# Attention and soft MoE on one core: the x transposes behind the routing, two masks in one matmul, and GpSimd's subtractions ahead of both spreads

## Chip, cores, metric

The kernel runs on one core of a Trainium2 chip. The metric is the device time of one execution in microseconds; lower is better. The core has the engines PE (matmul, with its weight loads PEld), VectorE (DVE), ScalarE (ACT), GpSimd (POOL) and SyncE (SP), which here issues transfers. Each engine runs its instructions in the order in which they are written; semaphores hold an instruction until what it needs is there.

## What is computed

Eight batches of causal attention with 12 heads of 448 positions and 64 dimensions; its output x (3584 x 768) goes through a soft mixture of 8 experts with 4 slots each. All is fp32.

```python
scores = scale * np.matmul(q, k.transpose(0, 1, 3, 2))
scores = np.where(mask, -1000000000.0, scores)
attn = np.exp(scores - np.max(scores, axis=-1, keepdims=True))
attn = attn / (np.sum(attn, axis=-1, keepdims=True) + 1e-09)
x = np.matmul(attn, v)               # heads side by side: (3584, 768)
logits = x @ phi                     # (3584, 32)
d = np.exp(logits - logits.max(0))   # over all positions
slot_input = (d / (d.sum(0) + 1e-09)).T @ x
h = np.maximum(slot_input[e] @ w1[e], 0.0); slot_out[e] = h @ w2[e]
c = np.exp(logits - logits.max(1, keepdims=True))
out = (c / (c.sum(1, keepdims=True) + 1e-09)) @ slot_out
```

## The kernel before

The attention part is a loop over 48 blocks, `block(p)` (lines 505 to 590); a block finishes one pair of heads, a = 2p and a + 1, and prepares the next pair. Six blocks are one batch; `m6 = p % 6`. Every instruction is kept in program order, so the order of the code is the order of each engine's queue.

Scores are kept transposed (keys in the partitions) in one of three PSUM buffers `s_[0..2]` of two banks each, head i in `s_[i % 3]`. They are made in two passes, since q and k are split into a rounded part and a rest. `scores1_all(i)` writes the causal masks with matmuls of the bf16 tile `tri` against an identity, and adds the products of the rounded parts for the four key chunks k3 (64 columns), k2 (192), k1 (320) and k0 (448). `max_keys(i, 0..2)` reduces the finished first pass on VectorE to a maximum per query (tile `r`: one large reduction with a transpose, two small ones). `max_row` transposes that on PE into `rt` and takes the last maximum on VectorE (`mr`). `max_spread` spreads it on GpSimd into the first 14 rows of `r2`. `scores2(i)` then adds with four matmuls the rests of q and the subtracted maximum. `exps` makes the exponential on ScalarE (`pt`). `attv` and `attv3` multiply by v: 64 matmuls for a pair, into `po`. `norm` divides on VectorE: steps 0 and 1 make the reciprocal `sm` of the row sums, step 2, in the next block, writes x.

For the routing, `xtrans(p)` transposes x of a pair by four PE transposes into the bank of `po`, and ScalarE copies it to `xts`. `next_logits` multiplies two pairs' `xts` by phi, and VectorE adds that to `lt`; `logits_b`, `logits_d` and `logits_e` keep the running maximum and exponentials, `dispatch_a/b` sum x into the slots' inputs `si`. These use the score buffer `m = s_[(a + 1) % 3]`, which is free at the end of a block and becomes the buffer of the head after next.

The casts are ScalarE's: `cast_q` and `cast_k` round q and k into `qd` and `ks`, two buffers each, and `copy_k2` copies rounded k to `k2`. The rests are GpSimd's: `sub_k(p + 2)` and `sub_q(p + 2)`, into `ks` and `r2`. Raw q and k come by `load_qk` on SP's queue into four rotating buffers; a load waits there for the subtraction that read the buffer last, and v and a weight tile are loaded by the same queue ahead of them. `misc()` hands out one PSUM bank, used for `rt`.

In block p, PE's order is: `scores2(a)`, `scores1_all(a + 2)`, `xtrans(p - 1)`, `scores2(a + 1)`, `scores1_all(a + 3)`, `rt` of a + 2, the 64 products, `rt` of a + 3, then logits, dispatch or neither by `m6`. Behind the last block come the experts, which read weights as they are loaded, and the combination and output.

Of the kernel before, what the change touches and what calls it, by code (L numbers as in the profile page):

```python
# [17 lines left out]
P = 128  # L18
# [62 lines left out]
def attention_soft_moe(ctx: ExitStack, tc: tile.TileContext, qk, va, phi, w1, w2, out):  # L81
# [91 lines left out]
    for hs in (slice(0, 1), slice(1, 2)):  # L173
# [11 lines left out]
    nc.gpsimd.memset(ident, 0.0)  # L185
    nc.gpsimd.affine_select(out=ident, in_=ident, compare_op=ALU.not_equal, fill=1.0,
                            base=0, pattern=[[-1, P]], channel_multiplier=1)
    tri = const.tile([P, P], BF16, name="tri")
    nc.gpsimd.memset(tri, 0.0)
    nc.gpsimd.affine_select(out=tri, in_=tri, compare_op=ALU.is_ge, fill=NEG,  # L190
                            base=0, pattern=[[1, P]], channel_multiplier=-1)

    pob = ps_1.tile([P, 512], F32, name="po")
    po2 = pob[:, 0:NQ * VC].rearrange("p (a b)->p a b", b=VC)
# [14 lines left out]
    def misc(name):  # L209
        return ps_1.tile([P, 512], F32, tag="m", name=name)  # L210
# [37 lines left out]
    def scores1(i, part):  # L248
        if i >= NHD:
            return  # L250
        p, h = divmod(i, 2)
        ks, qd = ks_[p % NR], qd_[p % NR]
        if ("s", i) not in st:
            st["s", i] = s_[i % 3]
            st["open"] = set()
        s = st["s", i]

        bank = part in ("c12", "k1", "k2")
        start = bank not in st["open"]
        st["open"].add(bank)  # L260
        if part[0] == "k":
            c = int(part[1])
            o, w, m = S * h + P * c, S - CQ0[c], min(P, S - P * c + (KP if i else 0))
            nc.tensor.matmul(s[0:m, SCOL[c]:SCOL[c] + w], ks[:, o:o + m],
                             qd[:, h, CQ0[c]:S], start=start, stop=False, skip_group_check=True)
            return
        if part == "c12":
            o = s[:, SC1:SC1 + 2 * SC2].rearrange("p (a n) -> p a n", n=SC2)[:, :, 0:P]
            mask = tri.unsqueeze(1).to_broadcast([P, 2, P])
        else:  # L270
            w = P if part == "c0" else S - 3 * P
            o, mask = s[:, SCOL[int(part[1])]:SCOL[int(part[1])] + w], tri[:, 0:w]
        nc.tensor.matmul(o, identb, mask, start=start, stop=False, skip_group_check=True)

    def scores1_all(i):
        for part in ("c0", "c3", "k3", "c12", "k2", "k1", "k0"):
            scores1(i, part)

    def max_keys(i, k):
# [20 lines left out]
    def max_row(i, k, w=RW - RF):  # L300
        if i >= NHD:
            return
        if k == 0:
            st["rt", i] = misc(f"rt{i}")
            nc.tensor.transpose(out=st["rt", i][0:w, 0:P], in_=r_[i % 2][:, RF:RF + w], identity=ident)
        else:
            mr = st["mr", i] = wk.tile([NQB, 32], F32, tag="mr", name=f"mr{i}", bufs=2)
            nc.vector.tensor_reduce(out=mr, in_=st.pop(("rt", i))[0:NQB, 0:P].rearrange("p (g t)->p t g", g=4),
                                    axis=AX.X, op=ALU.max, negate=True)

    def max_spread(i):
        if i >= NHD:
            return
        p, h = divmod(i, 2)
        mr = st.pop(("mr", i))

        nc.gpsimd.affine_select(out=r2_[p % NR][0:NQB, h].rearrange("p (b t)->p b t", t=32),
                                in_=mr.unsqueeze(1).to_broadcast([NQB, NQB, 32]),
                                compare_op=ALU.is_equal, fill=0.0, base=0,
                                pattern=[[-1, NQB], [0, 32]], channel_multiplier=1)  # L320
# [144 lines left out]
    later = [lambda: nc.gpsimd.memset(mk, 0.0), lambda: nc.gpsimd.memset(mk[96:P, 64:P], -1.0e30),  # L465
             lambda: nc.gpsimd.memset(run_m[1], 3.0e38), lambda: nc.gpsimd.memset(run_z, 0.0),
             lambda: nc.gpsimd.memset(si, 0.0), lambda: nc.gpsimd.memset(sid, 0.0)]
    later += [lambda g=g: sid_part(g) for g in range(4)]
    later += [lambda: nc.gpsimd.memset(nm[:, 0:NSLOT], 0.0)]

    later += [lambda: nc.gpsimd.tensor_copy(out=srep, in_=sid.unsqueeze(1).to_broadcast([P, 4, NSLOT]))]

    warm(START[0], a=x_[1][:, NCH - 1, 0:AW].bitcast(BF16))
    h0, h1 = slice(0, 1), slice(1, 2)
# [9 lines left out]
        max_keys(0, k)  # L484
    cast_k(0, h1)
    cast_q(0, h1)
    sub_k(0, h1, nc.vector)
    max_row(0, 0)
    max_row(0, 1)
    max_spread(0)  # L490
    warm(START[2])
    scores1_all(1)
# [1 line left out]
    copy_k2(0, h0)  # L494
    cast_k(1, h0)
    cast_k(1, h1)
    cast_q(1, h0)
    sub_k(1, h0)
    sub_k(1, h1)
    for k in range(3):  # L500
# [4 lines left out]
    def block(p):  # L505
        a, b = 2 * p, p // 6 - 1
        last, m6 = p == NPAIR - 1, p % 6
        if p + 1 < NPAIR:
            loads_v(p + 1, nc.sync if p + 1 < NPAIR - 1 else nc.scalar)
        if p % 2 and p // 2 < RES - 1 or p == 2 * RES - 2:  # L510
            load_w(p // 2)
        load_qk(p + 3, 0)

        if p:
            norm(p - 1, 2)
        scores2(a, range(NCH))
        exps(a)
        if p == 0:
            max_row(1, 0)
            max_row(1, 1)  # L520
            max_spread(1)
            copy_k2(0, h1)
            cast_q(1, h1)
            sub_q(1)
        scores1_all(a + 2)
        for k in range(3):
            max_keys(a + 2, k)
        if p:
            cast_q(p + 2)
            xtrans(p - 1)  # L530
        scores2(a + 1, range(NCH))
        exps(a + 1)
        if p == 0:
            cast_k(2)
            cast_q(2)
# [12 lines left out]
        max_spread(a + 2)  # L548
        if p == 0:
            sub_q(2)  # L550
# [23 lines left out]
        m = s_[(a + 1) % 3]  # L574
        if m6 in (3, 5) and p > 6:
            dispatch_a(b, m6 // 5, m)
            dispatch_b(b, m6 // 5, m)
        elif m6 == 1 and p > 6:
            logits_e(b, m)
        elif m6 in (2, 4):  # L580
            next_logits(p // 6, m6 - 2, m)
            if p == NPAIR - 2:
                dispatch_a(b, 1, m[:, 512:1024])
                dispatch_b(b, 1, m[:, 512:1024])
        elif m6 == 0 and p:
            next_logits(b, 4, m)
            logits_b(b, lt)

    for p in range(NPAIR):
        block(p)  # L590
# [316 lines left out]
```

## Time and profile before

| | |
|---|---|
| median of 3 runs (lowest to highest) | 426.62 us (426.61 to 427.95) |
| the profiled execution: time, span | 427.31 us, 425.4 us |
| attention blocks | from 10.2 us to about 329 us of the span |
| share of the span, DVE, ACT, POOL | 70%, 67%, 62% |
| DMA, mean | 280 GB/s |
| ScalarE: exponential of one head, copy of `xts` | 1.03 us, 0.59 us |
| GpSimd: subtraction for a pair, spread of one head | 2.08 us, 0.64 us |

A row of the timeline has the start in microseconds from the span's start, the duration, the engine, line and operation, the tiles (out<-in), sizes and a count of instructions merged; in brackets stands how long the engine was idle before and what released it. All operations go through one helper, so all have line 65, and are told apart by their tiles. `s<-r,k` is `scores2`, `s<-tri,identb` are the masks, `s<-qd,ks` is `scores1`, `po<-ident,x` are the x transposes, `s<-xts,phi` the logits and `s<-x,gs` the dispatch. A matmul's duration includes its way through the array: starts of successive rows tell its pace.

### The profile page before, as it was taken

To read this page: it belongs to the slowest core of one execution; us is meant where nothing else is said; L and a number is where in the kernel's file an instruction comes from. 1 tells how busy PE (TensorE), PEld (TensorE's weight loads), DVE (VectorE), ACT (ScalarE), POOL (GpSimd) and SP (SyncE) were. 2 spreads that over 40 slices of the span, in tenths; PEclk is the share of its full clock that TensorE was granted. 3 is DMA by queue.
4 is the path that set the end of the run, shared out by engine and by line. 5 is a ranking of instruction groups with operands and counts; after the bars stand their busy time and mean duration, and the time that the engine had idled before them with its cause. 6 is when DMAs were issued, how large, how long until landed. Compare 5 with 4: busy or idle time off the path is not lost.

```text
span 425.4 us, 14150 instructions
## 1 busy us (share of the span) xinstructions
PE 382.2 (90%) x5752; PEld 288.2 (68%) x5752; DVE 296.9 (70%) x817; ACT 283.6 (67%) x400; POOL 265.8 (62%) x215
## 2 busy tenths in 40 slices
PE   6689999999999999999999999999997998998840
PEld 3577878777877778787787777787876654543430
DVE  7667787787787877878778788787785477423440
ACT  5778888788877978788788788787953111333330
POOL 7998888787887887888879787887851000000000
PEclk9999999999999999999999999999999999999995
DMA  7777786787767777668767777776769999999997
GB/s 274 244 226 250 251 280 182 243 267 249 241 204 242 256 266 251 222 219 273 257 232 210 237 264 230 260 254 197 285 230 331 378 422 422 425 418 414 394 384 319
DMA packets 34480, 119.17 MB, mean 280 GB/s; under 512 B 3824, under 2 KB 8944, under 8 KB 32880
## 3 DMA queue, kind: packets, MB, share of 16 engines
q1 hardware_dynamic: 34272, 118.01, 78.4%
q8 instruction: 45, 0.74, 0.7%
q10 hardware_dynamic: 144, 0.27, 0.2%
q14 instruction: 19, 0.16, 0.1%
HBM read 107.25 MB, written 11.01 MB: 278 GB/s over the span
## 4 chain that ended last, share of the span: by engine, by line
PE 66%; DVE 18%; DMA 4%; issue 2%; ACT 1%; POOL 0%; DVEq 0%
PE po L65 29%; PE s L65 23%; DVE x L65 7%; PE rt L65 5%; DMA w<-in_w_dram 4%; PE so L65 2%; DVE si L65 2%; PE pp L65 2%; PE hp L65 2%; DVE lm L65 2%; DVE sm L65 1%; DVE mr L65 1%; DVE lg L65 1%; PE cp L65 1%; PE e L65 1%
## 5 line engine op out<-in xcount | busy, mean ns | idle before, releaser
L65 ACT ACTIVATE pt<-s 128x1024 f32<-128x1024 f32 x96 | 98.5, 1026 | 57.1 <-PE s L65 50.9
L65 DVE TRANSPOSE_TENSOR_REDUCE r<-s 128x32 f32<-128x1024 f32 x96 | 120.0, 1250 | 22.1 <-PE s L65 18.1
L65 POOL TENSOR_TENSOR r<-qk,qd 64x896 fp32r<-64x896 f32 (+1 forms) x48 | 100.0, 2083 | 11.8 <-ACT qd L65 6.5
L65 POOL TENSOR_TENSOR ks<-qk,ks 64x896 fp32r<-64x896 f32 (+1 forms) x48 | 98.9, 2060 | 4.2 <-ACT ks L65 0.5
L65 PE MATMUL po<-va,pt 128*64 128x65 f32 x3040 | 99.4, 223 | 0.2 <-ACT xts L65 0.2
L65 PEld LDWEIGHTS po<-va,pt 128*64 128x64 f32 x3040 | 92.8, 138 | 6.2 <-ACT xts L65 0.4
L65 POOL TENSOR_SCALAR_AFFINE_SELECT r<-mr 14x448 fp32r<-14x448 f32 x96 | 61.4, 640 | 39.9 <-DVE sm L65 30.2
L65 PE MATMUL s<-qd,ks 128*128 128x448 f32 (+4 forms) x384 | 78.2, 315 | 0.7 <-POOL ks L65 0.4
L65 PE MATMUL s<-r,k 128*128 128x448 f32 (+3 forms) x384 | 69.7, 303 | 3.5 <-POOL r L65 3.5
L65 PEld LDWEIGHTS s<-r,k 128*128 128x128 f32 (+1 forms) x384 | 55.9, 176 | 19.3 <-issue 12.5
L65 PEld LDWEIGHTS s<-qd,ks 128*128 128x128 f32 (+2 forms) x384 | 49.7, 181 | 1.0 <-POOL ks L65 0.6
L65 ACT ACTIVATE ks<-qk 128x896 fp32r<-128x896 f32 (+1 forms) x50 | 46.0, 922 | 6.3 <-DMA qk<-in_qk_dram 2.6
L65 DVE TENSOR_REDUCE mr<-rt 14x32 f32<-14x128 f32 x96 | 24.8, 258 | 36.4 <-PE rt L65 36.3
L65 ACT ACTIVATE qd<-qk 128x896 fp32r<-128x896 f32 (+1 forms) x50 | 45.9, 918 | 1.0 <-DMA qk<-in_qk_dram 1.0
L65 ACT ACTIVATE k<-ks 64x896 fp32r<-64x896 f32 (+1 forms) x49 | 45.8, 935 | 1.1
L65 PE MATMUL s<-tri,identb 128*128 128x128 bf16 (+2 forms) x288 | 42.7, 235 | 2.7
L65 PE MATMUL po<-ident,x 128*128 128x128 f32 x188 | 30.7, 286 | 8.1 <-DVE x L65 6.2
L65 DVE TENSOR_REDUCE r<-r 128x16 f32<-128x32 f32 x192 | 33.7, 176 | 5.0
L65 PEld LDWEIGHTS po<-ident,x 128*128 128x128 f32 x188 | 19.8, 140 | 22.5 <-DVE x L65 22.4
L65 PE MATMUL rt<-ident,r 128*76 128x128 f32 x96 | 27.5, 287 | 2.6 <-DVE r L65 2.5
L65 ACT ACTIVATE xts<-po 128x512 f32<-128x512 f32 x47 | 27.9, 594 | 2.4 <-PE po L65 1.3
L65 PEld LDWEIGHTS <-identb 128*128 128x128 bf16 x309 | 24.1, 99 | 6.8 <-issue 5.8
(138 smaller groups left out, 364.1 us busy)
## 6 DMA issues: line engine op xcount, KB each, us to landing
qk<-in_qk_dram SPq DMA_DIRECT2D x94, 448.0 KB, 5.0
w<-in_w_dram SPq DMA_DIRECT2D x43, 768.0 KB, 6.1
w<-in_w_dram SPq DMA_DIRECT2D x10, 1536.0 KB, 20.4
va<-in_va_dram SPq DMA_DIRECT2D x47, 260.0 KB, 2.9
out_dram<-ot SPq DMA_DIRECT2D x16, 384.0 KB, 6.7
out_dram<-ot SPq DMA_DIRECT2D x2, 1536.0 KB, 9.3
qk<-in_qk_dram SPq DMA_DIRECT2D x4, 224.0 KB, 3.4
hw<-in_w_dram SPq DMA_DIRECT2D x1, 768.0 KB, 6.3
```

Of the source, the lines that this page charges most:

```text
L65: return self._tc.keep_in_program_order(op(*args, **kwargs))
```

## The change

It has five parts.

- `xtrans(p - 1)` moves to the end of the block, behind logits and dispatch, and writes the bank of `misc()`; its copy is a function of its own, `xcopy`, called a block later behind `exps(a)`. The logits of a pair follow a block later, so `m6` shifts by one for all routing steps; the last block gets one set of logits and two copies more.
- `max_row(a + 3, 0)` goes ahead of `attv3`, the last 16 of the 64 products, and writes columns 512 to 639 of `m` instead of the bank of `misc()`.
- The masks of chunks 0 and 3 are one matmul of 192 columns, with a tile `tri2` that holds both; k3 comes behind both mask matmuls.
- GpSimd subtracts q of pair p + 1 and then k of pair p + 2, both ahead of the block's two spreads; the cast of q moves behind the second exponential and the copy of k2, and q's load behind its subtraction.
- At the start, GpSimd's work on `sid` and `srep` moves to the last block, two halves of casts are put together or moved, and k of pair 2 is subtracted on VectorE.

```diff
-    tri = const.tile([P, P], BF16, name="tri")
+    tri2 = const.tile([P, AW + P], BF16, name="tri2")
+    tri = tri2[:, AW:AW + P]
...
-            w = P if part == "c0" else S - 3 * P
-            o, mask = s[:, SCOL[int(part[1])]:SCOL[int(part[1])] + w], tri[:, 0:w]
+            o, mask = s[:, SC3:SC3 + AW + P], tri2
...
-        for part in ("c0", "c3", "k3", "c12", "k2", "k1", "k0"):
+        for part in ("c03", "c12", "k3", "k2", "k1", "k0"):
...
     def xtrans(p):
-        x = st.pop(("x", p))
+        x, xm = st.pop(("x", p)), misc(f"xm{p}")
+        st["xm", p] = xm
         for c in range(NCH):
-            nc.tensor.transpose(out=pob[:, P * c:P * c + P], in_=x[:, c], identity=ident)
+            nc.tensor.transpose(out=xm[:, P * c:P * c + P], in_=x[:, c], identity=ident)
+
+    def xcopy(p):
         xt = st["xt", p] = xtp.tile([P, 512], F32, tag="xt", name=f"xts{p}", bufs=XT)
-        nc.scalar.activation(out=xt, in_=pob, func=AF.Copy)
+        nc.scalar.activation(out=xt, in_=st.pop(("xm", p)), func=AF.Copy)
...
-        load_qk(p + 3, 0)
-
+
+        if last:
+            for f in last_of:
+                f()
...
+        elif p > 1:
+            xcopy(p - 2)
         scores1_all(a + 2)
...
-        if p:
-            cast_q(p + 2)
-            xtrans(p - 1)
+        if p == 0:
+            cast_k(2, h0)
         scores2(a + 1, range(NCH))
...
-        sub_k(p + 2)
-        load_qk(p + 4, 1)
+        sub_q(p + 1)
+        load_qk(p + 3, 0)
         if p:
-            sub_q(p + 2)
-        max_row(a + 2, 0)
-        if m6 == 1 and p > 6:
+            sub_k(p + 2)
+            load_qk(p + 4, 1)
+        if m6 == 2 and p > 6:
             logits_d(b, lt)
         copy_k2(p + 1)
+        cast_q(p + 2)
         cast_k(p + 3)
+        max_row(a + 2, 0)
...
+        if p == 0:
+            sub_k(2, eng=nc.vector)
+            load_qk(4, 1)
         begun = set()
         if last:
+            next_logits(p // 6, 2, s_[(a + 2) % 3])
+            xtrans(p - 1)
+            xcopy(p - 1)
...
+        m = s_[(a + 1) % 3]
+        max_row(a + 3, 0, AW, m[:, 512:512 + P])
         attv3(p)
-        max_row(a + 3, 0, AW)
...
+        if m6 == 1 and p > 1:
             next_logits(b, 4, m)
             logits_b(b, lt)
+        elif m6 == 2 and p > 6:
+            logits_e(b, m)
+        elif m6 in (3, 5):
+            next_logits(p // 6, m6 - 3, m)
+        if m6 in (3, 4) and p > 6:
+            mm = m[:, 640:1024] if m6 == 3 else m[:, 0:384]
+            dispatch_a(b, m6 - 3, mm)
+            dispatch_b(b, m6 - 3, mm)
+        if p:
+            xtrans(p - 1)
```

In PE's queue, at the middle of block 4 before the change (`s_86` takes the first pass of head 10, `s_85` the second pass of head 9), the x transposes stand between the two heads:

```order
L65 MATMUL s_86<-qd_91,ks_92 128x192
L65 MATMUL s_86<-qd_91,ks_92 128x320
L65 MATMUL s_86<-qd_91,ks_92 128x448
L65 MATMUL po<-ident,x_94 128x128 x4
L65 MATMUL s_85<-r_90,k_97 128x448
L65 MATMUL s_85<-r_90,k_97 128x320
L65 MATMUL s_85<-r_90,k_97 128x192
L65 MATMUL s_85<-r_90,k_97 66x64
```

At the same place of the changed kernel, the second head's `scores2` follows directly:

```order
L65 MATMUL s_86<-tri_129,identb 128x2x128
L65 MATMUL s_86<-qd_91,ks_92 66x64
L65 MATMUL s_86<-qd_91,ks_92 128x192
L65 MATMUL s_86<-qd_91,ks_92 128x320
L65 MATMUL s_86<-qd_91,ks_92 128x448
L65 MATMUL s_85<-r_90,k_97 128x448
L65 MATMUL s_85<-r_90,k_97 128x320
L65 MATMUL s_85<-r_90,k_97 128x192
```

Nothing of the routing is left between the two heads, and k3 (66x64) now precedes k2.

PE's queue at the end of block 4, which has logits, before (the last of the 64 products, `rt` of the second head, logits of two pairs, next block):

```order
L65 MATMUL po<-va_93,pt_99 64x65
L65 MATMUL po<-va_93,pt_101 64x65
L65 MATMUL rt_710<-ident,r_96 64x128
L65 MATMUL s_85<-xts_556,phi_151 32x128 x4
L65 MATMUL s_85<-xts_650,phi_152 32x128 x4
L65 MATMUL s_86<-r_98,k_97 128x448
```

In the changed kernel, in block 5, which has logits now, `rt` of the second head stands between two runs of products:

```order
L65 MATMUL po<-va_100,pt_99 64x65 x12
L65 MATMUL po<-va_100,pt_101 64x65 x12
L65 MATMUL s_87<-ident,r_96 64x128
L65 MATMUL po<-va_100,pt_99 64x65
L65 MATMUL po<-va_100,pt_101 64x65
```

and at that block's end, from the last product on, stand:

```order
L65 MATMUL po<-va_100,pt_101 64x65
L65 MATMUL s_87<-xts_607,phi_154 32x128 x4
L65 MATMUL s_87<-xts_701,phi_155 32x128 x4
L65 MATMUL xm_788<-ident,x_94 128x128 x4
L65 MATMUL s_85<-r_90,k_97 128x448
```

The second head's `rt` stands 16 products earlier, in the score buffer, and the x transposes are the block's last work.

GpSimd's queue over one block and a half, before (`ks` and `r` with `qk` are the subtractions of k and q, `r<-mr` the spreads):

```order
L65 TENSOR_TENSOR ks_92<-qk_5_374,ks_92 64x896
L65 TENSOR_TENSOR r_98<-qk_5_427,qd_91 64x896
L65 AFFINE_SELECT r_90<-mr_579 14x448
L65 AFFINE_SELECT r_90<-mr_618 14x448
L65 TENSOR_TENSOR ks_89<-qk_6_468,ks_89 64x896
L65 TENSOR_TENSOR r_90<-qk_6_531,qd_88 64x896
```

And of the changed kernel:

```order
L65 TENSOR_TENSOR r_90<-qk_4_345,qd_88 64x896
L65 TENSOR_TENSOR ks_92<-qk_5_348,ks_92 64x896
L65 AFFINE_SELECT r_90<-mr_540 14x448
L65 AFFINE_SELECT r_90<-mr_578 14x448
L65 TENSOR_TENSOR r_98<-qk_5_437,qd_91 64x896
L65 TENSOR_TENSOR ks_89<-qk_6_440,ks_89 64x896
```

The subtraction of q is now that of pair 4 beside k of pair 5, and stands first; it writes the `r2` buffer that the block's spreads write too.

More of the change, by code (lines that the diff above doesn't have):

```diff
@@ L187, in attention_soft_moe @@
                             base=0, pattern=[[-1, P]], channel_multiplier=1)
-    tri = const.tile([P, P], BF16, name="tri")
-    nc.gpsimd.memset(tri, 0.0)
-    nc.gpsimd.affine_select(out=tri, in_=tri, compare_op=ALU.is_ge, fill=NEG,
-                            base=0, pattern=[[1, P]], channel_multiplier=-1)
+    tri2 = const.tile([P, AW + P], BF16, name="tri2")
+    tri = tri2[:, AW:AW + P]
+    nc.gpsimd.memset(tri2, 0.0)
+    for t in (tri2[:, 0:AW], tri):
+        nc.gpsimd.affine_select(out=t, in_=t, compare_op=ALU.is_ge, fill=NEG,
+                                base=0, pattern=[[1, t.shape[1]]], channel_multiplier=-1)
     pob = ps_1.tile([P, 512], F32, name="po")
@@ L298, in max_keys, with max_row @@
                                     axis=AX.X, op=ALU.max)
-    def max_row(i, k, w=RW - RF):
+    def max_row(i, k, w=RW - RF, to=None):
         if i >= NHD:
@@ L303, in max_row @@
         if k == 0:
-            st["rt", i] = misc(f"rt{i}")
+            st["rt", i] = misc(f"rt{i}") if to is None else to
             nc.tensor.transpose(out=st["rt", i][0:w, 0:P], in_=r_[i % 2][:, RF:RF + w], identity=ident)
@@ L466, in attention_soft_moe @@
              lambda: nc.gpsimd.memset(run_m[1], 3.0e38), lambda: nc.gpsimd.memset(run_z, 0.0),
[L467 to L471, printed above, removed]
+             lambda: nc.gpsimd.memset(si, 0.0)]
+    last_of = [lambda: nc.gpsimd.memset(sid, 0.0)]
+    last_of += [lambda g=g: sid_part(g) for g in range(4)]
+    last_of += [lambda: nc.gpsimd.memset(nm[:, 0:NSLOT], 0.0)]
+    last_of += [lambda: nc.gpsimd.tensor_copy(out=srep, in_=sid.unsqueeze(1).to_broadcast([P, 4, NSLOT]))]
     warm(START[0], a=x_[1][:, NCH - 1, 0:AW].bitcast(BF16))
@@ L486, in attention_soft_moe @@
     cast_q(0, h1)
-    sub_k(0, h1, nc.vector)
     max_row(0, 0)
     max_row(0, 1)
+    sub_k(0, h1, nc.vector)
     max_spread(0)
@@ L496, in attention_soft_moe @@
     cast_k(1, h1)
-    cast_q(1, h0)
+    cast_q(1)
     sub_k(1, h0)
@@ L522, in block @@
             copy_k2(0, h1)
-            cast_q(1, h1)
-            sub_q(1)
+        elif p > 1:
+            xcopy(p - 2)
         scores1_all(a + 2)
@@ L533, in block @@
         if p == 0:
-            cast_k(2)
-            cast_q(2)
+            cast_k(2, h1)
         scores1_all(a + 3)
         max_keys(a + 3, 0)
-        sub_k(p + 2)
-        load_qk(p + 4, 1)
+        sub_q(p + 1)
+        load_qk(p + 3, 0)
         if p:
-            sub_q(p + 2)
-        max_row(a + 2, 0)
-        if m6 == 1 and p > 6:
+            sub_k(p + 2)
+            load_qk(p + 4, 1)
+        if m6 == 2 and p > 6:
             logits_d(b, lt)
         copy_k2(p + 1)
+        cast_q(p + 2)
         cast_k(p + 3)
+        max_row(a + 2, 0)
         max_row(a + 2, 1)
         max_spread(a + 2)
-        if p == 0:
-            sub_q(2)
         for k in (1, 2):
             max_keys(a + 3, k)
+        if p == 0:
+            sub_k(2, eng=nc.vector)
+            load_qk(4, 1)
         begun = set()
         if last:
+            next_logits(p // 6, 2, s_[(a + 2) % 3])
+            xtrans(p - 1)
+            xcopy(p - 1)
             attv(a, [(qc, qc, FULL if qc < 3 else FULL[0:1]) for qc in range(NCH)], po0, begun)
@@ L572, in block @@
             norm(p, k)
[L574 to L585, printed above, removed]
+        if m6 == 1 and p > 1:
             next_logits(b, 4, m)
             logits_b(b, lt)
+        elif m6 == 2 and p > 6:
[8 more added lines that the diff above has]
+            xtrans(p - 1)
     for p in range(NPAIR):
```

## The prediction

> **What bounds the kernel now.** I read the page first, for which engine is full and until when, then the waits, then one block and six blocks of the timeline.
>
> ```profile
> PE 382.2 (90%) x5752; PEld 288.2 (68%) x5752; DVE 296.9 (70%) x817; ACT 283.6 (67%) x400; POOL 265.8 (62%) x215
> PE   6689999999999999999999999999997998998840
> DMA  7777786787767777668767777776769999999997
> ```
>
> PE is busy 90% of the span. The second and third lines are forty slices of 10.6 us: PE is at 9 tenths from slice 4 to slice 30; that is the attention part, 48 blocks of one pair of heads. After it the transfers are at 9 tenths, so the last quarter streams weights and moves as a whole with the end of attention. What the change is worth is read from a block. Is a full PE also the limit? The waits answer:
>
> ```profile
> DVE mr L65 <- PE rt L65: 36.3, 48, 1.2
> POOL r L65 <- DVE sm L65: 30.2, 45, 0.9
> PEld po L65 <- DVE x L65: 22.4, 45, 1.2
> PEld s L65 <- POOL r L65: 4.6, 5, 1.3
> ```
>
> Columns: total us, times, longest. Weight loads for the x transposes wait 22.4 us for VectorE over 45 blocks; GpSimd holds PE up only 5 times. So the exchange between PE and VectorE decides. Here is one block, from its first `scores2` (I call that moment 0) at 150.52 to the next at 157.12:
>
> ```profile
> 150.52 0.73 PE L65 MATMUL s<-r,k 128*128 128x448 f32 x4
> 151.09 0.26 PE L65 MATMUL s<-tri,identb 128*128 128x128 bf16 x2
> 151.30 0.72 PE L65 MATMUL s<-qd,ks 128*128 128x192 f32 x3
> 151.40 0.57 DVE L65 TENSOR_SCALAR x<-po,sm 64x64 f32<-64x64 f32 x2
> 152.03 0.66 PE L65 MATMUL po<-ident,x 128*128 128x128 f32 x4
> 152.05 1.25 DVE L65 TRANSPOSE_TENSOR_REDUCE r<-s 128x32 f32<-128x1024 f32 x1
> 152.44 0.71 PE L65 MATMUL s<-r,k 128*128 128x448 f32 x4
> 153.34 0.40 DVE L65 TENSOR_REDUCE r<-r 128x16 f32<-128x32 f32 x2
> 153.88 0.28 PE L65 MATMUL rt<-ident,r 128*76 128x128 f32 x1
> 154.00 1.25 DVE L65 TRANSPOSE_TENSOR_REDUCE r<-s 128x32 f32<-128x1024 f32 x1 [0.27 <-PE s L65]
> 154.10 2.09 PE L65 MATMUL po<-va,pt 128*64 128x65 f32 x64
> 155.34 0.37 DVE L65 TENSOR_REDUCE r<-r 128x16 f32<-128x32 f32 x2
> 156.11 0.30 PE L65 MATMUL rt<-ident,r 128*64 128x128 f32 x1
> 156.34 0.85 PE L65 MATMUL s<-x,gs 128*32 128x384 f32 x8
> 157.12 0.73 PE L65 MATMUL s<-r,k 128*128 128x448 f32 x4
> ```
>
> The first head's scores end at 152.02; VectorE starts on them at 152.05 and needs 1.25 and 0.40 us, till 153.74; PE's transpose `rt` of these maxima starts 0.14 later, at 153.88, and the 64 products with v stand behind it. So **a fixed chain runs from the block's start to `rt`**: scores, two reductions, handover, 3.36 us. Beside the reductions PE does three things: the x transposes (152.03 to 152.44, 0.41 us), the second head's `scores2` and its `scores1` (152.44 to 153.88, at most 1.44 us with any wait).
>
> The chain is longer where VectorE or the mask matmuls come late:
>
> ```profile
> 158.00 0.25 PE L65 MATMUL s<-tri,identb 128*128 128x128 bf16 x2
> 160.76 0.28 PE L65 MATMUL rt<-ident,r 128*76 128x128 f32 x1
> 163.79 0.73 PE L65 MATMUL s<-r,k 128*128 128x448 f32 x4
> 177.05 0.73 PE L65 MATMUL s<-r,k 128*128 128x448 f32 x4
> 180.93 0.28 PE L65 MATMUL rt<-ident,r 128*76 128x128 f32 x1
> 183.42 0.72 PE L65 MATMUL s<-r,k 128*128 128x448 f32 x4
> 183.94 0.27 ACT L65 ACTIVATE lg<-s 128x128 f32<-128x128 f32 x1
> 184.26 0.24 PE L65 MATMUL s<-tri,identb 128*128 128x128 bf16 x2
> 187.09 0.28 PE L65 MATMUL rt<-ident,r 128*76 128x128 f32 x1
> ```
>
> Leads from block start to `rt`: 3.36 for the block at 150.52 (B), 3.64 at 157.12 (C; its masks wait 0.3 us longer for VectorE's read of the dispatch sums), 3.88 at 177.05 (F; x comes late behind the logits' reductions), 3.67 at 183.42 (A; ScalarE's `lg` copy leaves the bank only at 184.21). The two blocks from 163.79 to 177.05 take 13.26, as B and C together (6.60 + 6.67). One batch of six thus has leads of 2 x 3.36 + 2 x 3.64 + 3.88 + 3.67 = 21.55 us.
>
> **The change, part by part.** *x transposes to the end of the block.* They leave the stretch in which VectorE reduces, but the chain to `rt` does not get shorter by it: PE arrives there 0.41 us earlier and waits for the same reductions. At the block's end nothing runs beside them that PE would have waited for: they cost four steps of 0.41 / 4 us, 0.41 per block, in 45 blocks (pairs 2 to 46): **+18.5 us**. The cover that they lose is the reduction; the cover that they give is to VectorE's and ScalarE's reads of the bank behind logits and dispatch, which now have 0.41 us more before the next masks. With that the leads of C and F fall to 3.36. A stays at 3.67: ScalarE's queue in front of `lg` (two exponentials, x copy, three casts, the logits' own) is as long as before, and `lg` still comes last in it. New leads of six: 5 x 3.36 + 3.67 = 20.47, so 1.08 saved in six blocks, times 45 / 6: **-8.1 us**. VectorE has no reason to start earlier than 1.53 us into a block, since the scores that it reads end there.
>
> *The second head's `rt` inside the products*, ahead of the last 16 of 64. Its reductions end 1.71 us after their start (154.00 to 155.71) and now start right behind the first head's, at about 3.2, so are done at 4.9 to 5.0; PE is there at 3.36 + 0.22 + 48 x 0.03 = 5.0 us. No wait to speak of, and a row of products is interrupted once more. Step from `rt` to products is 0.22 (153.88 to 154.10) or, at the least, one product (2.09 / 64 = 0.03); step from products to logits the same 0.03 or the 0.23 from `rt` to the dispatch (156.11 to 156.34), which goes. Net between 0.03 + 0.03 - 0.23 = -0.17 and 0.22 + 0.23 - 0.23 = +0.22 per block, -7.7 to +9.9 us in 45. Middle near zero, and the shape of this `rt` (128*64) is that of the products: I take **0**.
>
> *Two masks in one matmul.* The same columns are streamed (128 + 64 + 256); one start goes, and the 64-column k3 now stands behind both masks, directly ahead of a 128-column load. Only the first head's copy lies on the chain. The two masks and k3 take 151.09 to 151.30 with the 256-wide one, 0.21 us; a third of that, 0.07, is the most that one start fewer can save or a badly hidden load can cost: 0, bounds -3 to +3 us. The Trainium skill, "TensorE: Matmul & The Clock Gate", section on LDWEIGHTS, has a load take its columns over 1.2 ns, which hides only behind a matmul of that length; for k3's 64 columns ahead of 128 that speaks against the new order. As an estimate from that page some 0.05 us would show per head, and the sum would be 2 us higher.
>
> *GpSimd.* Order per block: sub_q, sub_k, two spreads; before: sub_k, sub_q, two spreads, with sub_q for a pair further on.
>
> ```profile
> L65 POOL TENSOR_TENSOR r<-qk,qd 64x896 fp32r<-64x896 f32 (+1 forms) x48 | 100.0, 2083 | 11.8 <-ACT qd L65 6.5
> L65 POOL TENSOR_SCALAR_AFFINE_SELECT r<-mr 14x448 fp32r<-14x448 f32 x96 | 61.4, 640 | 39.9 <-DVE sm L65 30.2
> 7.32 1.88 POOL L65 TENSOR_SCALAR_AFFINE_SELECT sid<-sid 128x32 f32<-128x32 f32 x4
> 18.79 0.74 PE L65 MATMUL s<-r,k 128*128 128x448 f32 x4 [1.06 <-POOL r L65]
> 21.68 0.73 PE L65 MATMUL s<-r,k 128*128 128x448 f32 x4 [0.95 <-POOL r L65]
> 26.63 0.62 PE L65 MATMUL s<-r,k 128*128 128x448 f32 x2 [1.11 <-POOL r L65]
> qk<-in_qk_dram SPq DMA_DIRECT2D x94, 448.0 KB, 5.0
> 322.68 0.85 PE L65 MATMUL s<-x,gs 128*32 128x384 f32 x8 [0.48 <-DVE lt L65]
> ```
>
> Two subtractions and two spreads are 2 x 2.08 + 2 x 0.64 = 5.44 us of a block of 6.6: GpSimd keeps a microsecond free, and sub_q no longer waits for a cast of the same block (6.5 us in all). Worth nothing on the path in the steady part. q is held a block longer, so its next load is issued a block later on SP's queue, behind sub_q; it lands in 5.0 us (the median) and is cast a block later, over 6.6 us after issue: 0. ScalarE's cast of q moves behind the second exponential; what needs it is now the next block's scores and no longer a subtraction of the same block: 0. **At the start** it does count: the 1.88 us of `sid` work leave GpSimd's queue for the last block, where it idles, and sub_k of pair 2 goes to VectorE. PE's three waits there are 1.06 + 0.95 + 1.11 = 3.12 us; the products and reductions of the same blocks are close behind, so I take two thirds, **-2.0 us**, bounds -3.1 and 0.
>
> *The end.* Block 46 loses PE's wait of 0.48 us between logits and dispatch; the last block gets a set of logits and two x copies ahead of its products, and weights can follow q's buffers only half a block later. I take **+0.5**, bounds -0.5 and +2.
>
> Sum: 18.5 - 8.1 + 0 + 0 - 2.0 + 0.5 = **+8.9 us**, on the profiled execution's 427.31 us (span 425.4). That execution lies 0.7 above the median of 426.62; with the same difference the median becomes 435.5.
>
> **Rivals.** *The transposes were in the way (faster).* Place: `rt` of the first head. If the reductions were through 0.41 us earlier, 1.28 instead of 1.69 us behind the scores, PE would not wait there, every lead would be 3.36 - 0.41 = 2.95, and six blocks would save 21.55 - 17.70 = 3.85, 28.9 in 45: 18.5 - 28.9 - 2.0 + 0.5 = -11.9, **414.7 us**. For it: the 22.4 us that PE waits for x go. Against: `rt` starts 0.14 behind the second reduction, in a block where x was no hindrance, and 1.25 + 0.40 repeat in every block. Chance 0.12.
>
> *The split products cost nothing and drop the old step (no change).* The lower bound above, -7.7: **427.8 us**. For: equal tile shapes. The Trainium skill, "TensorEngine Tiling (Array Packing)", Key Properties, says that a change of tiling mode drains the array; by it `rt` among products of its own shape would be free. Against: between this `rt` and the dispatch, and between the other `rt` and the products, the trace shows steps of 0.23 and 0.22. Chance 0.12.
>
> *A new wait behind the split (slower still).* The maxima's transpose now lies in the same buffer as the logits, so logits and dispatch must follow VectorE's read `mr`, one more step PE-VectorE-PE: 36 blocks with logits, dispatch or both, up to 0.3 us each beyond the 16 products that cover it, +10.8: **446.3 us**. For: VectorE's reads of `rt` start late (36.3 us of waits). Against: 16 products and a step take about 0.7 us, which is nearly such a round. Chance 0.14.
>
> That the change doesn't do what it says: the order of instructions shows that it does.
>
> **How the numbers follow.** Forecast 0.62 at 435.5 us. A measurement of this kernel tells about 0.3% (1.3 us) from no change. Faster: the first rival and a third of the second, 0.16; same: 0.05 out of the second; slower: the rest, 0.79. The range leaves out the first rival and the upper half of the third: 427.0 to 446.5, which also takes in the bounds -7.7 and +9.9 of the split.
>
> **What would show it.** Right: behind the second `scores1` a PE wait for VectorE's `r` of about half a microsecond per block, in place of the waits for x, at an unchanged lead of 3.36; transposes of 0.41 at the block's end with no wait; blocks of nearly 7 us with logits, 6.2 without. Wrong: a lead near 3.0; or a step of PE around the second `rt` well off 0.4 us in sum. In the first 27 us the waits for GpSimd should be gone.

## The result, and the profile after

The changed kernel takes 444.37 us (median of 4 runs, 443.75 to 445.01), beside 427.09 us for the kernel before (4 runs): a ratio of 1.0402, 95% interval 1.0377 to 1.0427. It is slower by 17.3 us; 8.9 were forecast. The profiled execution took 444.26 us, with a span of 442.6.

The page of the changed kernel, first PE's line in the list of engines, then PE in forty slices of the span (11.1 us each), then three groups of PE's instructions (busy us, mean ns, and behind the second bar the idle time before them):

```profile
PE 382.8 (86%) x5656; PEld 296.3 (67%) x5656; DVE 299.5 (68%) x818; ACT 283.7 (64%) x400; POOL 262.6 (59%) x215
...
PE   7798898989889898998989898898989899999750
...
L65 PE MATMUL s<-r,k 128*128 128x448 f32 (+3 forms) x384 | 64.5, 290 | 0.3 <-POOL r L65 0.3
...
L65 PE MATMUL rt<-ident,r 128*76 128x128 f32 x49 | 13.5, 276 | 31.4 <-DVE r L65 30.8
...
L65 PE MATMUL xm<-ident,x 128*128 128x128 f32 x188 | 30.5, 284 | 0.0
```

PE does almost the same work (382.8 us of it, 382.2 before) in a span 17.2 us longer, so what grew is PE's idle time and the steps between its rows. It changes between 8 and 9 tenths all through the attention part, where it stood at 9. The group of `rt` has the new idle time: the first head's `rt` waits 30.8 us for VectorE's maxima. The x transposes wait for nothing.

Among the waits of the changed kernel (total us, times, longest), these answer to those shown of before:

```profile
POOL r L65 <- DVE mr L65: 72.2, 93, 4.1
...
PE rt L65 <- DVE r L65: 30.8, 47, 1.5
...
PE s L65 <- DVE lt L65: 2.9, 7, 0.4
```

PE's weight loads no longer wait for VectorE's x. GpSimd, through with both subtractions, waits for the maxima before each spread, 72.2 us in all; it is early, and PE waits for it 0.3 us in all (the group of `scores2`, `s<-r,k`, above).

One block with logits in the timeline (PE and VectorE), from its first `scores2` at 129.50 to the next at 136.45 (6.95 us), without the first passes of the scores:

```profile
129.50 0.71 PE L65 MATMUL s<-r,k 128*128 128x448 f32 x4
...
130.84 0.63 PE L65 MATMUL s<-r,k 128*128 128x448 f32 x4
131.03 1.25 DVE L65 TRANSPOSE_TENSOR_REDUCE r<-s 128x32 f32<-128x1024 f32 x1 [0.23 <-PE s L65]
...
132.32 0.40 DVE L65 TENSOR_REDUCE r<-r 128x16 f32<-128x32 f32 x2
132.86 0.28 PE L65 MATMUL rt<-ident,r 128*76 128x128 f32 x1 [0.61 <-DVE r L65]
133.07 1.62 PE L65 MATMUL po<-va,pt 128*64 128x65 f32 x48
134.62 0.30 PE L65 MATMUL s<-ident,r 128*64 128x128 f32 x1
134.85 0.69 PE L65 MATMUL po<-va,pt 128*64 128x65 f32 x16
135.47 0.64 PE L65 MATMUL s<-xts,phi 128*32 128x128 f32 x16
136.04 0.66 PE L65 MATMUL xm<-ident,x 128*128 128x128 f32 x4
136.45 0.72 PE L65 MATMUL s<-r,k 128*128 128x448 f32 x4
```

The lead is 3.36 us, as in block B before, with 0.61 us of idling ahead of `rt`; the x transposes take 136.04 to 136.45, 0.41 us, at the end. Both are as forecast. What was not: from the start of the products to the logits it now takes 133.07 to 135.47, 2.40 us; before it took 154.10 to 156.34, 2.24 us, from the products to the dispatch. The split row of products costs 0.16 us net in this block, where I had put 0.

One kind of block has a wait that was not forecast, the one with logits and a dispatch (PE and VectorE, some rows):

```profile
162.45 0.64 PE L65 MATMUL s<-xts,phi 128*32 128x128 f32 x16
...
163.16 0.29 DVE L65 TENSOR_TENSOR lt<-s,mk 128x128 f32<-128x128 f32 x1 [0.20 <-PE s L65]
163.50 0.85 PE L65 MATMUL s<-x,gs 128*32 128x384 f32 x8 [0.41 <-DVE lt L65]
```

VectorE reads the logits from columns 0 to 127 of the buffer `m`; the dispatch writes columns 640 to 1023 of the same buffer, and starts 0.05 us after that read's end, 0.41 us late. The third wait above is this one: seven times, 2.9 us.

Summed over the 45 blocks of pairs 2 to 46, from the starts of PE's rows in both traces: the leads to `rt` shrink from 161.6 to 152.1 us (-9.5); the x transposes at the end add 18.2; what lies between `rt` and these grows from 135.2 to 145.9 (+10.7).

The last can be read kind by kind, each beside the same kind of block before. The 29 blocks with logits, dispatch or both (waits for `lt` set aside) are 0.15 us longer in the mean; nine with no routing (two before) 0.29; the seven with the two transposes of `logits_e` 0.38, of which 0.25 lie ahead of these transposes. They differ because the step behind the second `rt`, which the split does away with, was 0.23 only in the first kind. Before, it was 0.08 ahead of the next block's `scores2` and 0.14 ahead of the transposes of `logits_e`:

```profile
38.66 0.30 PE L65 MATMUL rt<-ident,r 128*64 128x128 f32 x1
38.74 0.74 PE L65 MATMUL s<-r,k 128*128 128x448 f32 x4
...
183.15 0.30 PE L65 MATMUL rt<-ident,r 128*64 128x128 f32 x1
183.29 0.27 PE L65 MATMUL s<-ident,gs 128*128 128x128 f32 x1
```

So the split costs 29 x 0.15 + 9 x 0.29 + 7 x 0.25 = 8.7 us, and the new waits 2.9. The other -0.9 of the 10.7 holds one set of logits that moved into the last block (-0.7), one such wait that was there before (-0.5), the seven pairs of `logits_e` transposes, 0.13 longer each (+0.9), and -0.6 that is unassigned.

### The profile page after: what moved, and what is told of

Its sections match the earlier page's. It is cut to its first block, busy times and chain, and to the rows that moved or that the text cites. A ratio compares the mean times of both kernels' runs of the same rounds, so it can differ in the third digit from the quotient of the medians.

```text
span 442.6 us, 13829 instructions
## 1 busy us (share of the span) xinstructions
PE 382.8 (86%) x5656; PEld 296.3 (67%) x5656; DVE 299.5 (68%) x818; ACT 283.7 (64%) x400; POOL 262.6 (59%) x215
## 4 chain that ended last, share of the span: by engine, by line
PE 54%; DVE 21%; DMA 13%; issue 5%; ACT 2%; POOL 2%; DVEq 0%; POOLq 0%; SPq 0%; ACTq 0%
PE po L65 23%; PE s L65 20%; DVE r L65 17%; DMA w<-in_w_dram 13%; PE xm L65 5%; PE rt L65 3%; DVE x L65 2%; PE pp L65 1%; DVE lt L65 1%; PE hp L65 1%; PE e L65 1%; POOL r L65 1%; ACT ot L65 1%; DMA qk<-in_qk_dram 1%; POOL ks L65 1%
## 5 line engine op out<-in xcount | busy, mean ns | idle before, releaser
L65 PE MATMUL po<-va,pt 128*64 128x65 f32 x3040 | 109.8, 225 | 0.0
L65 POOL TENSOR_SCALAR_AFFINE_SELECT r<-mr 14x448 fp32r<-14x448 f32 x96 | 61.9, 644 | 73.7 <-DVE mr L65 72.2
L65 PEld LDWEIGHTS po<-va,pt 128*64 128x64 f32 x3040 | 96.6, 137 | 11.5 <-issue 0.2
L65 PE MATMUL s<-r,k 128*128 128x448 f32 (+3 forms) x384 | 64.5, 290 | 0.3 <-POOL r L65 0.3
L65 PE MATMUL rt<-ident,r 128*76 128x128 f32 x49 | 13.5, 276 | 31.4 <-DVE r L65 30.8
L65 PEld LDWEIGHTS rt<-ident,r 128*76 128x76 f32 x49 | 5.6, 115 | 45.7 <-ACT pt L65 41.1
L65 DVE TENSOR_REDUCE mr<-s 14x32 f32<-14x128 f32 x47 | 13.1, 279 | 33.2 <-PE s L65 32.5
L65 PE MATMUL s<-tri,identb 128*128 128x192 bf16 x192 | 34.7, 262 | 0.1
L65 PE MATMUL xm<-ident,x 128*128 128x128 f32 x188 | 30.5, 284 | 0.0
L65 PEld LDWEIGHTS xm<-ident,x 128*128 128x128 f32 x188 | 20.1, 140 | 12.6 <-issue 11.9
L65 ACT ACTIVATE xts<-xm 128x512 f32<-128x512 f32 x47 | 27.8, 592 | 0.2 <-PE xm L65 0.2
```

The source lines that it names most:

```text
L65: return self._tc.keep_in_program_order(op(*args, **kwargs))
```

## The experiments

Each ran beside the kernel before on the same chip; the medians of before were 427.07, 427.67, 427.74 and 427.86 us in the four batches. These medians lie up to 0.8 us apart, and the changed kernel's 444.37 us is from a batch of its own, so a smaller difference from it says nothing. A diff is against the changed kernel unless it says otherwise.

**The second `rt` among the products, alone** (a diff of the kernel before):

```diff
-    def max_row(i, k, w=RW - RF):
+    def max_row(i, k, w=RW - RF, to=None):
...
-            st["rt", i] = misc(f"rt{i}")
+            st["rt", i] = misc(f"rt{i}") if to is None else to
...
         for h in range(2):
             attv(a + h, [(qc, 3 * h + qc, FULL) for qc in range(3)], po2, begun)
+        m = s_[(a + 1) % 3]
+        max_row(a + 3, 0, AW, m[:, 512:512 + P])
         attv3(p)
-        max_row(a + 3, 0, AW)
...
-        m = s_[(a + 1) % 3]
```

> The kernel before, with one part of the change: the second head's rt into the score buffer, ahead of the last 16 products. Theory A (an interrupted row of products costs a step on each side, as the changed kernel's trace shows: 0.15 us net in blocks with logits or dispatch, 0.30 us in blocks with the two ident transposes): five blocks in six at 0.15 and one at 0.30, 0.175 x 45 = +7.9 us, about 435 us. Theory B (the prediction's zero: what the split adds on one side it saves on the other): 427 us, within 1.5.

Measured: 438.03 us, ratio 1.025 (1.0229 to 1.0272), 11.0 us slower than before. The split alone is no even trade. Two successive blocks of its timeline:

```profile
124.52 1.62 PE L65 MATMUL po<-va,pt 128*64 128x65 f32 x48
126.25 0.30 PE L65 MATMUL s<-ident,r 128*64 128x128 f32 x1
126.48 0.69 PE L65 MATMUL po<-va,pt 128*64 128x65 f32 x16
127.10 0.65 PE L65 MATMUL s<-xts,phi 128*32 128x128 f32 x16
...
131.24 1.62 PE L65 MATMUL po<-va,pt 128*64 128x65 f32 x48
132.86 0.30 PE L65 MATMUL s<-ident,r 128*64 128x128 f32 x1
```

From the 48 products to `rt` it takes 1.73 and 1.62 us, against 1.55 in the changed kernel: with the x transposes still between the heads the reductions of the second head end later, and `rt` comes 0.18 and 0.07 us too early for them. Over the 45 blocks the stretch from `rt` to the next block grew by 13.6 us and the leads fell by 2.7. Of the 13.6, an estimate with the prices of the next run gives about 7.7 to the split itself; the rest, 0.13 per block in the mean, is in line with such early `rt`.

**One more interruption of the products**, a transpose of 64 columns (`third_64`) or 76 columns (`third_76`) after the first 24 of the 48:

```diff
+        m = s_[(a + 1) % 3]
         for h in range(2):
             attv(a + h, [(qc, 3 * h + qc, FULL) for qc in range(3)], po2, begun)
-        m = s_[(a + 1) % 3]
+            if h == 0 and a + 3 < NHD:
+                nc.tensor.transpose(out=m[0:64, 512:512 + P], in_=r_[a % 2][:, RF:RF + 64], identity=ident)
```

> The changed kernel with one more transpose of 64 columns (a copy of the first head's, into the same place of the score buffer, overwritten by the second head's) in the middle of the first 48 products. Theory A (an interruption of the products costs a step on both sides, 0.15 and 0.23 us by the changed kernel's trace, for one of 0.03): 0.35 x 45 = +15.8 us, about 460 us. Theory B (it costs what the array needs for its 128 columns, 0.11 us, as between the x transposes): +5 us, about 449 us.

> The same with 76 columns, the shape of the first head's rt and not that of the products. Theory A (any interruption costs the same): as third_64 within 1 us. Theory B (a change of tile shape drains the array, one of the same shape doesn't; the Trainium skill, TensorEngine Tiling (Array Packing), Key Properties, speaks of a drain when the tiling mode changes): clearly more than third_64, by 0.1 us or more per block, 5 us.

Measured: 462.35 us (1.0819, 1.0787 to 1.0851) and 462.5 us (1.0813, 1.0787 to 1.084); both 18 us above the changed kernel, 0.38 in each of 47 blocks. One block of `third_64`, then the same rows of `third_76`:

```profile
108.35 0.28 PE L65 MATMUL rt<-ident,r 128*76 128x128 f32 x1 [0.60 <-DVE r L65]
108.55 0.92 PE L65 MATMUL po<-va,pt 128*64 128x65 f32 x24
109.40 0.30 PE L65 MATMUL s<-ident,r 128*64 128x128 f32 x1
109.63 0.92 PE L65 MATMUL po<-va,pt 128*64 128x65 f32 x24
110.48 0.30 PE L65 MATMUL s<-ident,r 128*64 128x128 f32 x1
110.71 0.69 PE L65 MATMUL po<-va,pt 128*64 128x65 f32 x16
111.32 0.65 PE L65 MATMUL s<-xts,phi 128*32 128x128 f32 x16
```

```profile
109.80 0.92 PE L65 MATMUL po<-va,pt 128*64 128x65 f32 x24
110.65 0.30 PE L65 MATMUL s<-ident,r 128*76 128x128 f32 x1
110.88 0.92 PE L65 MATMUL po<-va,pt 128*64 128x65 f32 x24
```

These rows price the split. From start to the next row's start, 24 products take 0.85 us and 48 take 1.55: 24 more cost 0.70, 0.029 each, so each run of products has a fixed 0.85 - 24 x 0.029 = 0.15 us besides. The 16 products fit (0.15 + 16 x 0.029 = 0.61; 110.71 to 111.32 is 0.61), and so do the 64 before (0.15 + 64 x 0.029 = 2.01). An interruption thus costs a second 0.15 and the step of 0.23 from the transpose back to the products: 0.38, which is what the times show. In the change it replaces the old step behind `rt`: 0.38 - 0.23 = 0.15 net ahead of logits or dispatch, 0.38 - 0.08 = 0.30 where nothing follows, 0.38 - 0.14 = 0.24 ahead of the `logits_e` transposes. The traces gave 0.15, 0.29 and 0.25. The width of the transpose changes nothing: 0.85 and 0.23 in both.

**The x transposes twice**, at the block's end, or a second set ahead of the first head's `rt` into a bank of its own:

```diff
-        for c in range(NCH):
+        for c in range(NCH * (1 if p == NPAIR - 2 else 2)):
+            c %= NCH
```

```diff
         cast_k(p + 3)
+        if p and not last:
+            w = misc(f"xw{p}")
+            for c in range(NCH):
+                nc.tensor.transpose(out=w[:, P * c:P * c + P], in_=st["x", p - 1][:, c], identity=ident)
         max_row(a + 2, 0)
```

> The changed kernel with the four x transposes at the block's end made twice, into the same bank. Theory A (nothing covers them there): 0.41 us in 45 blocks, +18.4 us, about 463 us. Theory B (the next block's start is set by VectorE or GpSimd, and PE only fills time): less than 5 us, below 449 us.

> The changed kernel with four more x transposes (of the x that is there since the block's start) ahead of the first head's rt, where the trace shows PE waiting 0.6 us for VectorE's r. Theory A (PE is idle there): no more than 1 us, 444 to 445.5 us. Theory B (PE's rows only look like a wait, the array is full): +18 us, about 463 us.

Measured: 464.21 us (1.0873, 1.0846 to 1.0901), 19.8 above the changed kernel, and 444.45 us (1.0405, 1.0377 to 1.0432), 0.1 above it. The same work costs 0.43 us per block (46 blocks) at the end and nothing ahead of `rt`. The timeline of the second:

```profile
136.03 0.72 PE L65 MATMUL s<-r,k 128*128 128x448 f32 x4
...
138.63 0.60 PE L65 MATMUL xw<-ident,x 128*128 128x128 f32 x4
139.40 0.28 PE L65 MATMUL rt<-ident,r 128*76 128x128 f32 x1 [0.18 <-DVE r L65]
```

Four transposes more stand ahead of `rt`, the lead stays at 3.37 us, and the idling falls from 0.61 to 0.18.

**The second `rt` behind all products, still in the logits' buffer**:

```diff
         m = s_[(a + 1) % 3]
+        attv3(p)
         max_row(a + 3, 0, AW, m[:, 512:512 + P])
-        attv3(p)
```

> The changed kernel with the second head's rt behind all 64 products again, still in the score buffer. Theory A (the split hides VectorE's read of rt, which logits and dispatch wait for since they lie in the same buffer): blocks with neither get 0.25 us shorter, the others 0.35 to 0.4 us longer: 1.7 us in six blocks, +13 us, about 457 us. Theory B (the split only costs): 0.18 x 45 = -8 us, about 436 us.

Measured: 456.82 us (1.0687, 1.0672 to 1.0702), 12.4 above the changed kernel. A block with logits:

```profile
138.45 0.30 PE L65 MATMUL s<-ident,r 128*64 128x128 f32 x1
139.22 0.65 PE L65 MATMUL s<-xts,phi 128*32 128x128 f32 x16 [0.47 <-DVE mr L65]
```

The wait that my third rival had for the changed kernel exists here: the logits wait 0.47 us for VectorE's `mr`, though they write other columns, and PE has 30 such waits, 14.2 us in all. The changed kernel has none; there the last 16 products cover that read. So undoing the split alone is worse, since the buffer of `rt` was changed with it.

**One routing step per block**: the first half's dispatch goes to the block after, the second half's to the first block of the next batch. In this run and in `routing_window` below, the dispatch reads part of x after the next batch's x has begun to take its place, so the slots' inputs are not those of the reference; the instructions and their sizes are the same.

```diff
-        if m6 in (3, 4) and p > 6:
-            mm = m[:, 640:1024] if m6 == 3 else m[:, 0:384]
-            dispatch_a(b, m6 - 3, mm)
-            dispatch_b(b, m6 - 3, mm)
+        for n, hf in ((b, 0), (b, 1)) if p == NPAIR - 2 else ((b, 0),) if m6 == 4 and p > 6 else ((b - 1, 1),) if m6 == 0 and p > 6 else ():
+            if n >= 0:
+                mm = m[:, 640:1024] if hf else m[:, 0:384]
+                dispatch_a(n, hf, mm)
+                dispatch_b(n, hf, mm)
```

> The changed kernel with the second half's dispatch of each batch moved from the block that has logits and dispatch to an empty one (m6 = 0 of the next batch; the last batch excepted). Theory A (PE's 0.41 us wait for VectorE's lt in those blocks is lost time): 6 x 0.41 = -2.5 us, about 442 us. Theory B (the wait covers what would be waited for later): 444.4 us within 1.

Measured: 442.51 us (1.0355, 1.0338 to 1.0372), 1.9 us less than the changed kernel. No PE wait for `lt` is left among its waits. That bears out the wait of 0.41 us, at two thirds of its 2.9. The remainder comes back in block 46, which makes both dispatches in this run and waits twice, 0.95 us in all:

```profile
335.58 0.85 PE L65 MATMUL s<-x,gs 128*32 128x384 f32 x8 [0.21 <-DVE mr L65]
337.17 0.85 PE L65 MATMUL s<-x,gs 128*32 128x384 f32 x8 [0.74 <-DVE si L65]
```

**The masks apart again**, k3 between them as before:

```diff
-            o, mask = s[:, SC3:SC3 + AW + P], tri2
+            w = P if part == "c0" else S - 3 * P
+            o, mask = s[:, SCOL[int(part[1])]:SCOL[int(part[1])] + w], tri[:, 0:w]
...
-        for part in ("c03", "c12", "k3", "k2", "k1", "k0"):
+        for part in ("c0", "c3", "k3", "c12", "k2", "k1", "k0"):
```

> The changed kernel with the masks as before: chunk 0, chunk 3, k3, chunks 1 and 2. Theory A (the same columns, only the first head's copy on the path): 444.4 us within 1.5. Theory B (the Trainium skill, TensorE: Matmul & The Clock Gate, section on LDWEIGHTS: the short k3 ahead of a 128-column load costs 0.05 us): about 2 us less, 442 us.

Measured: 443.25 us (1.0379, 1.0359 to 1.0399), 1.1 below the changed kernel; the two intervals overlap. In its timeline a lead is 128.58 to 131.91, 3.33 us, where the changed kernel has 3.36; over the 45 blocks its leads sum to 150.9 us instead of 152.1. So the masks' new form and k3's new place cost about 0.03 us of lead per block together, 1.2 us in all; the run undoes both at once and can't tell them apart. The Trainium skill, "TensorE: Matmul & The Clock Gate", section on LDWEIGHTS, has a load take its columns over 1.2 ns, from which the estimate of 0.05 us per head for k3's place was made. The sign agrees and the measured 0.03 us stands in its place; that the load is the cause is not shown.

**The start**: `sid` and `srep` back in GpSimd's queue ahead of the blocks, and, apart from that, k of pair 2 back on GpSimd:

```diff
+    later, last_of = later + last_of, []
```

```diff
         if p == 0:
-            sub_k(2, eng=nc.vector)
+            sub_k(2)
```

> The changed kernel with GpSimd's work on sid and srep at the start again. Theory A (it sets the first spreads): 1.5 to 2 us more, about 446 us. Theory B (the gain of the start comes from the other moved pieces): 444.4 us within 0.7.

> The changed kernel with the k of pair 2 subtracted on GpSimd, between the first two spreads of block 0. Theory A (this one subtraction is what the start gained): 2.1 us of GpSimd's queue ahead of the second spread, 1.5 to 2 us more, about 446 us. Theory B (the gain comes from the order of q and k): 444.4 us within 0.7.

Measured: 444.56 us (1.0396, 1.0381 to 1.041) and 444.94 us (1.0401, 1.0377 to 1.0426). Neither differs from the changed kernel. Block 2's first `scores2` in the changed kernel, then in the one with `sid` at the start:

```profile
25.07 0.72 PE L65 MATMUL s<-r,k 128*128 128x448 f32 x4
```

```profile
24.64 0.72 PE L65 MATMUL s<-r,k 128*128 128x448 f32 x4
```

Block 2 starts at 25.07 in the changed kernel (26.63 before) and no later with `sid` back. The waits for GpSimd at 18 to 26 us are gone, and neither of these two edits, taken back alone, brings them back; what remains are both together and the order of the casts and subtractions at the start, which were not tried.

**Routing in the idle time ahead of `rt`.** If the 0.61 us ahead of `rt` is free and the split is not, logits and dispatch belong there, in a bank of their own; the first `rt` then goes into `m`, and the second behind all products. Two versions: the first has one of logits or dispatch per block; the second has the changed kernel's own dispatch places, the masks apart, and the split kept only in the block of `logits_e`. The first's main lines:

```diff
-        max_row(a + 2, 0)
+        m = s_[(a + 1) % 3]
...
+            g = misc(f"g{p}")
...
+            logits_a(bb, (lg0, lg0 + 1), g[:, 0:P])
+        if ds0 is not None:
+            dispatch_a(*ds0, g[:, 0:384])
+        max_row(a + 2, 0, to=m[:, 0:P])
...
-        m = s_[(a + 1) % 3]
+        attv3(p)
         max_row(a + 3, 0, AW, m[:, 512:512 + P])
-        attv3(p)
```

> The changed kernel with logits and dispatch in the idle window ahead of the first head's rt (in the bank of misc, that rt in the score buffer, the second rt behind all products, one of logits or dispatch per block); x transposes stay at the end. Theory A (a fixed chain of 3.36 us with 0.6 us of PE idle in it): only what exceeds the window shows, 0.1 us for logits and 0.35 for a dispatch; blocks of 6.1 to 6.5 us, about 412 us. Theory B (VectorE's and ScalarE's queues in front of rt get longer by as much): 430 us or more.

> routing_window with both dispatches back in the blocks m6 = 3 and 4 (in m6 = 3 behind the logits, in the same window), the split of the products only in the blocks with the ident transposes, and the masks apart as before. If the window theory holds: 0.75 us more in 7 blocks, 0.06 less in others, 0.4 less in 7 blocks by the split, 0.03 less per block by the masks: 412 to 416 us, against about 427.4 before.

Measured: 414.56 us (0.9695, 0.9682 to 0.9708) and 413.84 us (0.9673, 0.9653 to 0.9692). The first lies 2.6 above its forecast of 412; the second is 3.3% faster than the kernel before. A block of the second with logits, PE's rows without the first passes, 119.07 to 125.22:

```profile
119.07 0.71 PE L65 MATMUL s<-r,k 128*128 128x448 f32 x4
...
120.37 0.63 PE L65 MATMUL s<-r,k 128*128 128x448 f32 x4
...
121.73 0.65 PE L65 MATMUL g<-xts,phi 128*32 128x128 f32 x16
122.50 0.28 PE L65 MATMUL s<-ident,r 128*76 128x128 f32 x1
122.71 2.09 PE L65 MATMUL po<-va,pt 128*64 128x65 f32 x64
124.73 0.30 PE L65 MATMUL s<-ident,r 128*64 128x128 f32 x1
124.86 0.60 PE L65 MATMUL xm<-ident,x 128*128 128x128 f32 x4
125.22 0.72 PE L65 MATMUL s<-r,k 128*128 128x448 f32 x4
...
128.66 0.28 PE L65 MATMUL s<-ident,r 128*76 128x128 f32 x1 [0.72 <-DVE r L65]
```

The block is 6.15 us long instead of 6.95. Its lead is 3.43, and so is, within 0.01, that of the next block (125.22 to 128.66), which has no routing and where PE idles 0.72 us ahead of `rt`. So the logits cost no lead here, instead of 0.57 us at the end (135.47 to 136.04); why every lead is some 0.08 longer than in the changed kernel was not followed up. The rest of the gain is the interruption that is gone and shorter steps around the second `rt` and the x transposes.

## Why the prediction was right and wrong

- **The bound** was right: a chain of scores, reductions and handover fixes the lead at 3.36 us, and PE idles ahead of `rt` (0.61 us in the timeline, 30.8 us in all, half a microsecond forecast). `x_twice_window` shows it: 0.41 us more of work there costs 0.1 us in the whole kernel. With that the first rival (faster, 414.7) falls: the lead did not shrink with the transposes gone.
- **x transposes at the end**, +18.5 forecast: 18.2 in the trace, and a second set costs 19.8.
- **The leads**, -8.1 forecast: -9.5. Five of six became 3.36 to 3.40 as forecast; the one kept at 3.67 (A's successor) became 3.43. ScalarE's `lg` copy no longer holds the masks up, against my step that it "still comes last".
- **The second head's `rt` inside the products**, 0 forecast with bounds -7.7 and +9.9: **this is the step that failed, a term that was mis-sized**. It is +8.7 us in the trace, and `split_only` is 11.0 us slower than before. The forecast counted steps between rows (0.03 to 0.23) and took the row of 64 products as 64 equal products. `third_64` shows that a run of products costs 0.15 us beyond its products, so cutting it in two costs that once more, plus a step back of 0.23, against an old step of 0.23, 0.14 or 0.08 that went. Blocks with no routing show it most plainly: 6.38 us each, where 6.2 was forecast. "Middle near zero" was a choice without a row; the shape of `rt`, by which I chose, plays no part (64 and 76 columns cost the same). That the measured time still lies within 427.0 to 446.5 us is due to the upper bound of this term, not to its middle.
- **A wait that was not in the sum**: 7 x 0.41 = 2.9 us, dispatch behind VectorE's read of the logits in the same buffer. Block 46 before had it once already, quoted at the end's term with 0.48; I read it as something that goes there and not as a price of each block that has both. Taking the wait out of those blocks gave 1.9 us.
- **Masks in one**, 0 with bounds of 3: +1.1 us in the time and +1.2 in the leads, at the edge of what these runs tell apart.
- **The rival with a new wait behind the split** (446.3) comes near the time, but by another mechanism: no PE wait for `mr` stands in the changed kernel. It appears when the 16 products no longer cover it (`unsplit`). Its 36 blocks also count the seven with `logits_e`; 29 have logits or dispatch. **The rival "split free"** falls. It drew on the Trainium skill, "TensorEngine Tiling (Array Packing)", Key Properties, for the drain at a change of tiling mode; whether such a drain lies inside the 0.15 us no run here shows, but a transpose of the products' own width was not free.
- **The start**, -2.0 forecast: block 2 starts 1.56 us earlier. The size was near and the reason is not borne out: putting back `sid` alone, or k of pair 2 alone, takes nothing of it away. **The end**, +0.5 forecast: from the last block's start to the end of the span it is 101.9 us before and 101.3 after, -0.6.

Sum with the measured sizes: 18.2 - 9.5 + 10.7 - 1.6 - 0.6 = 17.2 us, the difference of the two spans (442.6 - 425.4). Against the forecast's +8.9 that is 8.7 more for the split, 2.9 for the dispatch's wait and 0.4 at the start, and less 0.9 for the other items of the stretch behind `rt` and 2.8 for the leads, the end and the transposes (1.4 + 1.1 + 0.3).

## What to carry to other kernels

Before moving work out of a stretch, ask whether the engine would idle there: the x transposes stood in a wait for VectorE, where a second set of them costs nothing (`x_twice_window`), and the same idle time, filled with logits and dispatch, makes the kernel 3.3% faster than before. Price a cut through a run of short matmuls from two runs of different lengths: their difference gives the pace, and what is left is the fixed cost that each cut pays again. And where two steps share one buffer, look for a wait even if their columns differ.

## What the hardware showed that was not expected

- A run of n products of 64 x 65, fitted to 24 and 48 of them, took 0.15 + n x 0.029 us from its start to the next row's (n = 16, 24, 48, 64: 0.61, 0.85, 1.55, 2.01), and a transpose in its midst 0.38 us in all, equal for 64 and 76 columns. Which part of a run the 0.15 us lies in, the rows do not tell.
- PE's dispatch into columns 640 to 1023 of a PSUM buffer began only after VectorE had read columns 0 to 127 of it (0.41 us), and logits in columns 0 to 127 after its read of columns 512 to 639 (0.47 us). Whether this is the program's semaphores or the memory was not tried apart.
